# An RWKV-5 attention with a squared-ReLU feed-forward: the bonus term and the state's share of y computed in another way from unit 8, and the order written anew

## The chip, the cores and the metric

One Trainium2 chip, of which the kernel uses one core. The metric is the time of one execution on the device in microseconds (us). The profile is of one execution; its time is given beside its span, which runs from the first to the last instruction.

## The reference

```python
batch, n_heads, seq, head_dim = (4, 8, 768, 48)      # r, k, v; w and u are (heads, head_dim)
...
def _attn_ref(r, k, v, w, u):
    for t in range(S):
        kt, vt, rt = (k[:, :, t].copy(), v[:, :, t].copy(), r[:, :, t].copy())
        cur = np.einsum('bhd,bhe->bhde', u[None] * kt, vt)
        y[:, :, t] = np.einsum('bhd,bhde->bhe', rt, state + cur)
        state = w[None, :, :, None] * state + np.einsum('bhd,bhe->bhde', kt, vt)
...
def _moe_ref(x, w_in, w_out):                        # x is y as (3072, 384)
    h = x @ w_in                                     # w_in is (384, 2048)
    r = np.maximum(h, 0.0)
    g = r * r
    return (g @ w_out).astype(np.float32)            # w_out is (2048, 384)
```

The state of each head is a 48 x 48 matrix that decays by `w` at each step. The bonus term lets a token see itself with the weight `u`: it is the sum over d of r x u x k, one number for each token and head (the "diagonal sum"), times v.

## The kernel before

The sequence is cut into 6 chunks of 128 tokens; a chunk of one batch is a unit, 24 in all, numbered chunk by chunk with the four batches inside (unit 12 is chunk 3 of batch 0). A unit holds 128 tokens on the partitions and 8 heads of 48 numbers, 384 in all.

What is done for a unit i, by the names of the steps:

- `load` brings r, k and v. `scale` (VectorE) multiplies r and k by powers of w into a padded bf16 tile `rkw`, where each head has 64 places, so that a pair of heads fills 128. `cast_v` (ScalarE) makes v bf16.
- `turn` with `evict_rk` (units 0 to 5, on TensorE and ScalarE) or `turn_dma` (a transposing transfer) turns `rkw` to `rkT`, with the two heads of a pair on partitions 0 to 63 and 64 to 127.
- `at` (TensorE) computes the scores: 8 matmuls, each of 64 rows of the array, into two PSUM banks, even heads in one and odd heads in the other. `ats(i)` does that for units i and i + 1. `mask` (VectorE), two for a unit, reads one of these banks and writes the masked scores `am` as bf16.
- The diagonal sums: `rk` (VectorE) multiplies the turned r and k; four small matmuls in `sums` add it up over the partitions with the weights `uwb`. The same `sums` adds k^T v for the state (not for the last four units).
- `diag_v` (VectorE) multiplies v by the diagonal sums. `state_add`, `state_decay` (VectorE) bring the state up to date in `st32`. `state_cast` (ScalarE), two instructions of 64 partitions, copies it as bf16 into `stb`, whose 128 x 96 blocks have zeros off the diagonal.
- `y_mm` (TensorE): 8 matmuls of the masked scores with v, and from chunk 1 on 4 matmuls of the turned r with `stb`, into one bank. `evict_y` (VectorE) adds `diag_v`'s result and writes y as bf16. `x_turn` with `evict_x` (units 0 to 5) or `x_dma` turns y.
- The feed-forward: `mm1(i, m, s)` is TensorE's product with a part of `w_in`, for one unit (m = 1, 4 steps each) or two (m = 2, 8 steps for both); `relu` (ScalarE) reads the bank; `square` runs on VectorE or ScalarE as its last number says; `mm2(i, q)` is a quarter of the second product; `evict_o` (ScalarE) and `store` bring it out. The last unit's product is cut in two (`mm2_half`).

Nothing schedules this at run time. A long string, `SCHEDULE`, lists the steps in one order, and each engine runs its own instructions in that order; a word such as `ats:12@6,2,5,0` also names the PSUM banks (0 to 7) that the step takes. A bank is free again when its reader is done, and semaphores make the later step wait. `fill` steps are matmuls on constants that keep TensorE busy at the start.

Matmuls stand on `L434` (`mm1`), `L460` (`mm2`), `L475` (`mm2_half`), `L327` (`at`), `L347` and `L352` (`sums`), `L390` and `L396` (`y_mm`), `L310` (`turn`), `L420` (`x_turn`), `L232` (`fill`). On VectorE: `L287` (`scale`), `L319` (`rk`), `L339` (`mask`), `L361` (`diag_v`), `L369` and `L371` (`state_add`), `L375` (`state_decay`), `L405` (`evict_y`), `L453` (`square`). On ScalarE: `L442` (`relu`), `L451` (`square`), `L381` (`state_cast`), `L467` (`evict_o`). GpSimd issues some of the loads and nearly all stores, and computes a few small constants (`L259` among them); the other transfers are issued by SyncE (SP).

## Time and profile before

| | us |
|---|---|
| median of 3 runs | 174.15 |
| lowest, highest | 173.06, 174.81 |
| the profiled execution | 172.5 |
| its span | 170.4 |

The granted clock of TensorE is 1.000 of full speed throughout.

In the lines of the profile, `bank<-vb,am` says that an instruction writes a tile `bank` and reads `vb` and `am`; 128*128 is the part of the array that a matmul uses, and 128x96 the size of what it streams. A group's row gives the number of instructions, their busy time in us, the mean duration of one in ns, and behind the second bar the idle time of the engine before them with what ended it. A row of the timeline begins with the start and the length in us of a run of equal instructions. A row of waits gives total us, how often, and the longest. A row of the windows gives the stretch, its length, then the busy time of PE, PEld (the loading of weights), DVE (VectorE), ACT (ScalarE) and POOL (GpSimd), each with its count of instructions, and at last the clock, the share of the transfers and their GB/s.

### The profile page before, as it was taken

The numbers are of one execution on the slowest core, as the hardware profiler recorded it, in microseconds if no ns is written. First come the engines' busy times: TensorE is split into PE (matmuls) and PEld (weight loads), VectorE is DVE, ScalarE is ACT, GpSimd is POOL, SyncE is SP. The second block draws the span as 40 slices with busy tenths as digits, with TensorE's granted clock in tenths as the row PEclk, the third lists the DMA queues.
The fourth block names the chain that finished last, engine by engine and source line by source line (L and its number), as shares of the span: only waits on it lengthen the run. The fifth ranks groups of instructions, "written<-read, shape, count | busy, mean of one in ns | idle before, by whom it ended". The sixth has DMA issues, their size and how long they took to land.

```text
span 170.4 us, 4781 instructions
## 1 busy us (share of the span) xinstructions
PE 163.4 (96%) x1917; PEld 129.9 (76%) x1917; DVE 137.0 (80%) x297; ACT 120.9 (71%) x253; POOL 30.5 (18%) x62
## 2 busy tenths in 40 slices
PE   3899999999999999999999999999999999999993
PEld 2467998778778786795796895896898776999662
DVE  5359969969998999799988979988999898664800
ACT  3355489997685988579499499599359985295830
POOL 7989540000000500001100001203000030030010
PEclk9999999999999999999999999999999999999999
DMA  6999999989999999998999994998989994150014
GB/s 115 188 220 211 221 248 244 227 155 129 187 159 187 209 237 133 192 207 131 250 203 116 200 217 81 251 192 176 252 100 212 197 159 139 27 162 0 4 63 167
DMA packets 94784, 28.83 MB, mean 169 GB/s; under 512 B 90665, under 2 KB 92714, under 8 KB 94762
## 3 DMA queue, kind: packets, MB, share of 16 engines
q1 hardware_dynamic: 90512, 19.08, 73.9%
q0 software_dynamic: 4224, 9.44, 21.4%
q8 instruction: 15, 0.25, 0.6%
q14 instruction: 7, 0.06, 0.2%
q10 hardware_dynamic: 26, 0.00, 0.0%
HBM read 20.45 MB, written 4.72 MB: 148 GB/s over the span
## 4 chain that ended last, share of the span: by engine, by line
PE 84%; DVE 6%; DMA 5%; issue 1%; ACT 1%; ACTq 1%; DVEq 0%
PE bank L434 35%; PE bank L460 31%; PE bank L327 4%; DMA xT<-yb 3%; PE bank L390 3%; DMA rkT<-rkw 2%; PE bank L352 2%; PE bank L232 2%; PE bank L396 2%; PE bank L310 2%; PE bank L475 2%; DVE am L339 1%; DVE rkw L287 1%; PE bank L347 1%; DVE g L453 1%
## 5 line engine op out<-in xcount | busy, mean ns | idle before, releaser
L442 ACT ACTIVATE gr<-bank 128x512 f32<-128x512 f32 x96 | 53.1, 603 | 27.3 <-PE bank L434 25.9
L434 PE MATMUL bank<-xT,w_in_q 128*128 128x128 bf16 (+1 forms) x768 | 70.8, 246 | 0.6 <-DMA xT<-yb 0.4
L460 PE MATMUL bank<-w_out_q,g 128*128 128x384 bf16 x368 | 68.1, 327 | 0.1
L434 PEld LDWEIGHTS <-w_in_q 128*128 128x128 bf16 x768 | 64.2, 113 | 3.4 <-DMA xT<-yb 0.5
L460 PEld LDWEIGHTS <-g 128*128 128x128 bf16 x368 | 33.7, 98 | 19.2 <-DVE g L453 0.6
L453 DVE TENSOR_TENSOR g<-gr 128x512 bf16<-128x512 f32 x49 | 32.4, 686 | 6.9 <-ACT gr L442 6.8
L494 POOL DMA_DIRECT2D out_dram<-osb x21 | 11.3, 543 | 129.4 <-ACT osb L467 118.7
L339 DVE TENSOR_TENSOR am<-bank,smask 128x512 bf16<-128x512 f32 x48 | 31.4, 685 | 2.9 <-PE bank L327 2.8
L451 ACT ACTIVATE g<-gr 128x512 bf16<-128x512 f32 x47 | 29.1, 638 | 0.6
L287 DVE TENSOR_TENSOR rkw<-ldk,wneg 128x384 bf16<-128x384 f32 x24 | 13.2, 553 | 4.8 <-ACT wneg L240 3.6
L381 ACT CAST stb<-st 64x192 bf16<-64x192 f32 x40 | 13.9, 348 | 2.6 <-DVE st L375 2.3
L361 DVE TENSOR_TENSOR dv<-vb,bank 128x384 f32<-128x384 bf16 x24 | 13.0, 550 | 2.4 <-PE bank L352 1.5
L405 DVE TENSOR_TENSOR yb<-bank,dv 128x384 bf16<-128x384 f32 x24 | 13.3, 555 | 1.3 <-PE bank L396 0.3
L287 DVE TENSOR_TENSOR rkw<-ldr,wpos 128x384 bf16<-128x384 f32 x24 | 13.1, 553 | 1.0 <-DMA ldr<-in_r_dram 0.8
L319 DVE TENSOR_TENSOR rk<-rkT 128x512 bf16<-128x512 bf16 x24 | 10.0, 420 | 3.8 <-ACT rkT L314 2.0
L467 ACT COPY osb<-bank 128x384 f32<-128x384 f32 x23 | 10.5, 483 | 2.7 <-PE bank L460 2.7
L291 ACT CAST vb<-ldv 128x384 bf16<-128x384 f32 x24 | 12.1, 512 | 0.4 <-DMA ldv<-in_v_dram 0.3
L371 DVE TENSOR_TENSOR st<-bank,st 64x192 f32<-64x192 f32 x32 | 11.2, 351 | 1.2 <-PE bank L352 0.9
L232 PE MATMUL bank<-warm 128*128 128x256 bf16 x39 | 9.2, 334 | 2.0 <-DVE warm L183 1.5
L314 ACT COPY rkT<-bank 128x512 bf16<-128x512 bf16 x12 | 6.9, 595 | 3.7 <-PE bank L310 3.6
L390 PEld LDWEIGHTS <-am 128*128 128x128 bf16 x192 | 7.9, 96 | 2.0 <-issue 0.7
L327 PEld LDWEIGHTS <-rkT 64*128 64x128 bf16 x192 | 5.5, 96 | 4.2 <-issue 3.9
(58 smaller groups left out, 112.2 us busy)
## 6 DMA issues: line engine op xcount, KB each, us to landing
ldk<-in_k_dram SPq DMA_DIRECT2D x22, 192.0 KB, 4.6
out_dram<-osb POOLq DMA_DIRECT2D x21, 192.0 KB, 3.3
ldr<-in_r_dram SPq DMA_DIRECT2D x20, 192.0 KB, 3.7
ldv<-in_v_dram SPq DMA_DIRECT2D x19, 192.0 KB, 4.3
w_in_q<-in_moe_w_in_dram POOLq DMA_DIRECT2D x4, 384.0 KB, 8.9
w_out_q<-in_moe_w_out_dram POOLq DMA_DIRECT2D x4, 384.0 KB, 10.7
ldv<-in_v_dram POOLq DMA_DIRECT2D x5, 192.0 KB, 9.0
ldr<-in_r_dram POOLq DMA_DIRECT2D x4, 192.0 KB, 8.2
```

The costliest lines, as they stand in the source:

```text
L232: nc.tensor.matmul(out=banks[given.pop(0)][:, :n], lhsT=warm[:, :128], rhs=warm[:, :n], start=True, stop=True)
L287: nc.vector.tensor_tensor(t["rkw"][:, x, :, :, :D], pair(src), pair(wx), ALU.mult)
L339: nc.vector.tensor_tensor(am, t["at"][o], smask.unsqueeze(1).to_broadcast([C, HP, C]), ALU.mult)
L361: nc.vector.tensor_tensor(t["dv"], t["vb"], t["d"].unsqueeze(2).to_broadcast([C, H, D]), ALU.mult)
L381: nc.scalar.copy(stb[b][sl, :, o * D : (o + 1) * D], st32[b][sl])
L390: nc.tensor.matmul(out=y[:, 2 * p + o, :], lhsT=t[f"am{o}"][:, p, :], rhs=t["vb"][:, 2 * p + o, :], start=(o == 0 and p == 0), stop=c == 0 ...
L405: nc.vector.tensor_tensor(t["yb"], t["y"], t["dv"].rearrange("p h d -> p (h d)"), ALU.add)
L434: nc.tensor.matmul(out=t["h", s][:, a], lhsT=turned, rhs=chunks[c]["xT"][:, n, b : b + m, :], start=(n == 0), stop=(n == NK - 1),)
L442: nc.scalar.activation(t["gr", s], t["h", s], AF.Relu)
L451: nc.scalar.activation(g, x, AF.Square)
L453: nc.vector.tensor_tensor(g, x, x, ALU.mult)
L460: nc.tensor.matmul(out=t["o"], lhsT=chunks[units[i][0]]["g"][:, f, units[i][1], :], rhs=w_out_q[f // 4][:, f % 4, :], start=(f == 0), stop ...
```

## The change

From unit 8 on three things are computed in another way.

- The diagonal sums leave TensorE. `product` (VectorE) multiplies the scaled r and k in bf16 as they stand before the turn; `weigh` (GpSimd) multiplies that by u x w, spread over all partitions by two new loads (`wide_load`) and one product (`wide_product`); `fold` (GpSimd), twice, adds halves, 48 to 24 to 12 numbers a head; `head_sums` (VectorE) adds up the 12. `rk` and the four small matmuls of `sums` go.
- The state's share of y is computed inside `ats`, straight behind the scores: 16 matmuls for the two units, each of 64 rows and 48 columns, in place of 4 for a unit of 128 rows and 96 columns. Even and odd heads go to two banks, which the two units share, so `ats` takes six banks rather than four. `ys` later adds the masked scores' share for both units, and `evict_y` reads the two banks with two instructions. `state_cast` becomes one instruction of 128 partitions, into `stc`.
- The order is a new one for the whole kernel, from the start. By its words 65 squares run on ScalarE and 31 on VectorE (47 and 49 before), and there are 34 fills (39 before).

Of the string one line before and after, then the code:

```diff
-square:8:2:7:0 ats:12@6,2,5,0 store:5:POOL scale:14:0 mm2:9:2 mask:13:1 turn_dma:14 sums:13@7 mm1:10:2:0@1
...
+weigh:13 evict_o:7 load:17:rt:SP square:8:2:6:1 ats:12@5,7,0,4,3,6 turn_dma:15 square:8:2:7:1 state_decay:11 fold:13:0
...
+    WIDE_FROM = 8
     IN_PIECES, OUT_PIECES = (1, 1)
 
     const = ctx.enter_context(tc.tile_pool(name="const", bufs=1))
-    room = {"g": 2, "rkT": 5, "vb": 8, "rk": 3, "dv": 5, "yb": 4, "xT": 3, "gr": 6, "osb": 4, "am": 4}
+    room = {"pr": 4, "pw": 2, "ds": 4, "g": 2, "rkT": 5, "vb": 8, "rk": 3, "dv": 5, "yb": 4, "xT": 3, "gr": 6, "osb": 4, "am": 4}
     held = {"ldr": 6, "ldk": 8, "ldv": 6}
     pools = {}
 
@@ -218,6 +224,9 @@
     wend_c = const.tile([128, HP], F32)
     wend = wend_c.unsqueeze(2).to_broadcast([128, HP, D])
 
+    stc = [const.tile([128, HP, D], BF16, name=f"stc_{b}") for b in range(B)]
+    wide = [const.tile([128, H, D], F32, name=f"wide{x}") for x in range(2)]
+
     w_in_q = [const.tile([128, NK, dff // NQ], BF16, name=f"w_in_q{q}") for q in range(NQ)]
     w_out_q = [const.tile([128, NF // NQ, dm], BF16, name=f"w_out_q{q}") for q in range(NQ)]
 
@@ -312,6 +321,33 @@
     def evict_rk(i, x):
         t = tiles[i]
         nc.scalar.copy(turned(i)[:, x], t["tp", x])
+
+    def wide_load(x):
+        src = (w, u)[x].rearrange("h d -> (h d)").unsqueeze(0).to_broadcast([128, dm])
+        nc.sync.dma_start(out=wide[x].rearrange("p h d -> p (h d)"), in_=src)
+
+    def wide_product():
+        nc.gpsimd.tensor_tensor(wide[1], wide[1], wide[0], ALU.mult)
+
+    def product(i):
+        t = tiles[i]
+        t["pr"] = buffer("pr", [C, H, D], BF16)
+        nc.vector.tensor_tensor(pair(t["pr"]), t["rkw"][:, 0, :, :, :D], t["rkw"][:, 1, :, :, :D], ALU.mult)
+
+    def weigh(i):
+        t = tiles[i]
+        t["pw"] = buffer("pw", [C, H, D], F32)
+        nc.gpsimd.tensor_tensor(t["pw"], t["pr"], wide[1], ALU.mult)
+
+    def fold(i, n):
+        x = tiles[i]["pw"]
+        m = D >> (n + 1)
+        nc.gpsimd.tensor_tensor(x[:, :, :m], x[:, :, :m], x[:, :, m : 2 * m], ALU.add)
+
+    def head_sums(i):
+        t = tiles[i]
+        t["d"] = buffer("ds", [C, H], F32)
+        nc.vector.tensor_reduce(out=t["d"], in_=t["pw"][:, :, : D // 4], axis=mybir.AxisListType.X, op=ALU.add)
 
     def rk(i):
         t = tiles[i]
@@ -329,9 +365,21 @@
                     start=True, stop=True,
                 )
 
+    def halves(i):
+        return [bank("y", i - i % 2, o).rearrange("p (u x) -> p u x", u=2)[:, i % 2, : dm // 2].rearrange("p (a d) -> p a d", a=HP) for o in range(2)]
+
     def ats(i):
         at(i)
         at(i + 1)
+        for j in (i, i + 1):
+            y = halves(j)
+            for p in range(HP):
+                for o in range(2):
+                    sl = slice(o * 64, o * 64 + 64)
+                    nc.tensor.matmul(
+                        out=y[o][:, p, :], lhsT=tiles[j]["rkT"][sl, 0, p, :], rhs=stc[units[j][1]][sl, p, :],
+                        start=(j == i and p == 0), stop=False, skip_group_check=True,
+                    )
 
     def mask(i, o):
         t = tiles[i]
@@ -342,8 +390,9 @@
         c, b = units[i]
         t = tiles[i]
         t["s"] = bank("s", i)[:, :dm].rearrange("p (a d) -> p a d", a=HP)
-        t["d"] = bank("s", i)[:, dm : dm + H]
-        for p in range(HP):
+        if i < WIDE_FROM:
+            t["d"] = bank("s", i)[:, dm : dm + H]
+        for p in range(HP if i < WIDE_FROM else 0):
             nc.tensor.matmul(
                 out=t["d"], lhsT=t["rk"][:, p, :], rhs=uwb[:, p, :],
                 start=(p == 0), stop=(p == HP - 1 and c == NCH - 1), skip_group_check=True,
@@ -352,7 +401,7 @@
             nc.tensor.matmul(
                 out=t["s"][:, p, :], lhsT=t["rkw"][:, 1, p].rearrange("p o e -> p (o e)"),
                 rhs=t["vb"][:, 2 * p : 2 * p + 2, :].rearrange("p h d -> p (h d)"),
-                start=False, stop=(p == HP - 1), skip_group_check=True,
+                start=(i >= WIDE_FROM and p == 0), stop=(p == HP - 1), skip_group_check=True,
             )
 
     def diag_v(i):
@@ -376,9 +425,22 @@
 
     def state_cast(i):
         b = units[i][1]
-        for o in range(2):
+        if i >= WIDE_FROM - B:
+            nc.scalar.copy(stc[b], st32[b])
+        for o in range(2 if i < WIDE_FROM - B else 0):
             sl = slice(o * 64, o * 64 + 64)
             nc.scalar.copy(stb[b][sl, :, o * D : (o + 1) * D], st32[b][sl])
+
+    def ys(i):
+        for j in (i, i + 1):
+            t = tiles[j]
+            y = halves(j)
+            for p in range(HP):
+                for o in range(2):
+                    nc.tensor.matmul(
+                        out=y[o][:, p, :], lhsT=t[f"am{o}"][:, p, :], rhs=t["vb"][:, 2 * p + o, :],
+                        start=False, stop=j > i and p == HP - 1, skip_group_check=True,
+                    )
 
     def y_mm(i):
         c, b = units[i]
@@ -402,6 +464,12 @@
     def evict_y(i):
         t = tiles[i]
         t["yb"] = buffer("yb", [C, dm], BF16)
+        if i >= WIDE_FROM:
+            out_y = t["yb"].rearrange("c (a o d) -> c o a d", o=2, d=D)
+            dv = t["dv"].rearrange("c (a o) d -> c o a d", o=2)
+            for o, y in enumerate(halves(i)):
+                nc.vector.tensor_tensor(out_y[:, o], y, dv[:, o], ALU.add)
+            return
         nc.vector.tensor_tensor(t["yb"], t["y"], t["dv"].rearrange("p h d -> p (h d)"), ALU.add)
 
     def x_tile(i):
@@ -499,7 +567,8 @@
         evict_rk, evict_x, evict_y, fill, load, mask, mm1, mm2,
         mm2_half, power, relu, rk, scale, spread_columns, spread_log, square,
         state_add, state_cast, state_decay, store, store_half, sums, turn, turn_dma,
-        u_columns, win, wout, x_dma, x_turn, y_mm
+        u_columns, win, wout, x_dma, x_turn, y_mm, ys,
+        product, weigh, fold, head_sums, wide_load, wide_product
     )}
 
     def value(x):
```

More of the change, by code (lines that the diff above doesn't have):

```diff
@@ L108 @@
[L108 to L112 removed]
+load:1:kt:SP load:1:rt:POOL fill@7 load:0:rt:SP 2*fill@7 load:1:vt:POOL fill@7 load:0:kt:SP fill@7 load:2:kt:SP
@@ new lines @@
+relu:10:2:1 mm1:10:2:6@7 evict_y:13 state_cast:11 load:16:rt:SP square:10:2:2:1 mm2:8:1 product:15 x_dma:13
+relu:10:2:0 diag_v:12 mm2:8:2 weigh:15 square:10:2:1:1 evict_y:12 mm1:10:2:4@0 square:10:2:0:1 x_dma:12
+square:10:2:5:0 relu:10:2:6 sums:12@4 mm2:11:0@3 evict_o:9 state_add:12 fold:15:0 sums:13@6 relu:10:2:4 load:17:kt:SP
+mm2:11:1 weigh:14 state_add:13 state_cast:10 load:14:vt:SP relu:10:2:7 mm2:8:3 square:10:2:4:0 square:10:2:6:1
+load:18:kt:SP ats:14@7,1,4,0,6,5 evict_o:8 fold:14:0 load:18:rt:SP cast_v:15 store:6:POOL mm2:10:0@2 mask:15:0
```

187 lines of the change are left out of this document (93 added, 94 removed).

## The prediction

> **What bounds the kernel now.** I read the page first: busy times, then the chain of waits.
>
> ```profile
> span 170.4 us, 4781 instructions
> ...
> PE 163.4 (96%) x1917; PEld 129.9 (76%) x1917; DVE 137.0 (80%) x297; ACT 120.9 (71%) x253; POOL 30.5 (18%) x62
> ...
> PE 84%; DVE 6%; DMA 5%; issue 1%; ACT 1%; ACTq 1%; DVEq 0%
> ```
>
> The kernel is bound by TensorE. A busy PE says little, since a matmul's row covers its latency; what a step costs is the distance to the next step's start. The timeline of PE gives these prices:
>
> ```profile
> 86.86 0.36 PE L390 MATMUL bank<-vb,am 128*128 128x48 bf16 x8
> 87.06 0.33 PE L396 MATMUL bank<-stb,rkT 128*128 128x96 bf16 x4
> 87.23 0.25 PE L347 MATMUL bank<-uwb,rk 128*128 128x8 bf16 x4
> 87.33 0.33 PE L352 MATMUL bank<-vb,rkw 128*128 128x96 bf16 x4
> 87.50 0.81 PE L460 MATMUL bank<-w_out_q,g 128*128 128x384 bf16 x4
> 88.15 0.36 PE L390 MATMUL bank<-vb,am 128*128 128x48 bf16 x8
> ...
> 88.52 0.82 PE L434 MATMUL bank<-xT,w_in_q 128*128 128x256 bf16 x6
> 89.17 1.50 PE L460 MATMUL bank<-w_out_q,g 128*128 128x384 bf16 x8
> ...
> 93.21 0.62 PE L327 MATMUL bank<-rkT 64*128 64x128 bf16 x16
> 93.76 1.47 PE L460 MATMUL bank<-w_out_q,g 128*128 128x384 bf16 x8
> ```
>
> So y from the masked scores costs 0.20 us (86.86 to 87.06), y from the state 0.17, the four small diagonal matmuls 0.10, the state sums 0.17, an `mm2` quarter 0.65, an `mm1` step of two units 0.65, an `ats` 0.55. The start gives the rest, and the last row where PE ends:
>
> ```profile
> 19.45 0.83 PE L434 MATMUL bank<-xT,w_in_q 128*128 128x128 bf16 x12
> 20.12 0.33 PE L420 MATMUL bank<-identb,yb 128*128 128x128 bf16 x3
> 20.29 0.39 PE L310 MATMUL bank<-identb,rkw 128*128 128x128 bf16 x4
> 20.51 2.17 PE L434 MATMUL bank<-xT,w_in_q 128*128 128x128 bf16 x36
> ...
> 24.18 0.40 PE L327 MATMUL bank<-rkT 64*128 64x128 bf16 x8
> 24.51 0.30 PE L434 MATMUL bank<-xT,w_in_q 128*128 128x128 bf16 x2
> ...
> 164.79 2.80 PE L475 MATMUL bank<-w_out_q,g 128*128 128x256 bf16 x32
> ```
>
> An `mm1` step of one unit is 0.67 us, an `x_turn` 0.17, a `turn` 0.22, a single `at` 0.33. Useful work by counts of the steps: `mm1` 32 x 0.67 + 64 x 0.65 = 63.0; `mm2` 92 x 0.65 + 2.8 for the two halves = 62.6; `at` 8 x 0.33 + 8 x 0.55 = 7.0; diagonal and sums 24 x 0.10 + 20 x 0.17 = 5.8; y 24 x 0.20 + 20 x 0.17 = 8.2; turns 12 x 0.22 + 6 x 0.17 = 3.7. Together 150.3 of 170.4. PE ends at 167.6, so 2.8 is the tail. By 20.12 only 6 us of useful work is done (three units' turns, scores, sums and y, three `mm1` steps), so 14 is the start. That leaves about 3 us lost in the 147 us between: a new order can win hardly more than that there. Who is next in line is told by one long window:
>
> ```profile
> 60.00:140.00 80.00, 79.38 (x885) 63.63 (x883) 72.58 (x152) 62.46 (x133) 6.25 (x12) 1.00 1.11 184
> ```
>
> The columns after the length are PE, PEld, DVE, ACT and POOL busy. VectorE has 7.4 us free in these 80; it feeds PE through the masks.
>
> **The change part by part.** *PE.* Per pair from unit 8, two times 0.10 (diagonal) and two times 0.17 (state y) go: 0.54 us. In come 16 matmuls of 64 rows and 48 columns. The nearest row is `at`, also 64-row tiles: the second eight of an `ats` add 0.55 - 0.33 = 0.22, 27.5 ns each, so 16 x 27.5 = 0.44 us. The bounds are half of that, 0.22, if two row tiles of 48 columns share a slot, and a whole `ats`, 0.55. Saving per pair 0.10 (from -0.01 to 0.32), times 8: **-0.8 us** (+0.1 to -2.6). I keep 0.44, since `L390` with the same 48 columns also starts every 25 ns. The Trainium skill, "TensorE: Matmul & The Clock Gate", Part 3, says that matmuls in different row groups run together, starting about 4 ns apart; by that rule the 16 would be eight slots and the saving the upper one. The trace agrees in so far as the 128-column tiles of `at` come every 27.5 ns, and shows no 48-column row tile.
>
> *VectorE and ScalarE.* The groups:
>
> ```profile
> L453 DVE TENSOR_TENSOR g<-gr 128x512 bf16<-128x512 f32 x49 | 32.4, 686 | 6.9 <-ACT gr L442 6.8
> ...
> L451 ACT ACTIVATE g<-gr 128x512 bf16<-128x512 f32 x47 | 29.1, 638 | 0.6
> ...
> L381 ACT CAST stb<-st 64x192 bf16<-64x192 f32 x40 | 13.9, 348 | 2.6 <-DVE st L375 2.3
> ...
> L405 DVE TENSOR_TENSOR yb<-bank,dv 128x384 bf16<-128x384 f32 x24 | 13.3, 555 | 1.3 <-PE bank L396 0.3
> ...
> L319 DVE TENSOR_TENSOR rk<-rkT 128x512 bf16<-128x512 bf16 x24 | 10.0, 420 | 3.8 <-ACT rkT L314 2.0
> ...
> L371 DVE TENSOR_TENSOR st<-bank,st 64x192 f32<-64x192 f32 x32 | 11.2, 351 | 1.2 <-PE bank L352 0.9
> ...
> L375 DVE TENSOR_TENSOR st<-st,wend_c 128x192 f32<-128x192 f32 x16 | 5.6, 352 | 0.1
> ```
>
> Per unit from 8: `rk` goes (0.42). `product` comes, 384 bf16 elements: 0.36, between three quarters of `rk` (0.31) and `L405`'s 0.55 for 384 elements at full width. `head_sums` reads 96 elements: 0.25, at most `L375`'s 0.35. `evict_y` becomes two instructions of 192 elements: 2 x 0.351 against 0.555, +0.15. Net +0.34 x 16 = +5.4. `diag_v` stays at 384 elements. By the counts 18 squares leave VectorE (49 to 31): -18 x 0.66 = -11.9. So VectorE loses 6.5 (137.0 to about 130.5). ScalarE gets the 18 at 0.62 (29.1 / 47), +11.1, and casts 16 states in one instruction instead of two; `L375` against `L371` shows that 64 and 128 partitions cost the same, so -16 x 0.348 = -5.6: 126.4. Neither reaches PE; both are covered by PE's work as a sum. In units 8 to 21 VectorE has 10 squares less and 14 x 0.34 more: its 7.4 us of room become about 9.
>
> *GpSimd.* Per unit one product of 384 elements and two adds of 192 and 96. The trace has no such row; the nearest, by groups and by line (least, median and longest duration):
>
> ```profile
> masks.py:199 POOL TENSOR_SCALAR_AFFINE_SELECT identb<-identb 128x128 bf16<-128x128 bf16 x1 | 0.3, 292 | 0.1
> ```
> ```profile
> L259 POOL TENSOR_TENSOR wend_c<-wend_c x6: 192/198/470, 11.9 to 13.5; 128x4 f32<-128x4 f32 x6
> ```
>
> A product of four elements takes 198 ns (the median), a one-input operation on 128 takes 292: (292 - 198) / 124 = 0.76 ns an element. An estimate of twice that for two inputs, on 0.2 fixed, gives 0.78, 0.49 and 0.35: 1.6 us a unit, 26 in all (17 by the one-input rate, 35 by three times it). GpSimd goes from 30 to about 57 of 170, and it also issues the stores, so a store waiting for its `evict_o` holds up the weighting behind it. `head_sums` stands in VectorE's queue and waits for GpSimd; behind it stand squares, `scale`, `product` and `evict_y`. This is the place, pair 12 and 13 on VectorE, before:
>
> ```order
> L339 TENSOR_TENSOR am1_1722<-bank0_61,smask_134 128x512
> L375 TENSOR_TENSOR st32_3_139<-st32_3_139,wend_c_148 128x192
> L339 TENSOR_TENSOR am1_1741<-bank2_63,smask_134 128x512
> L339 TENSOR_TENSOR am0_1752<-bank5_66,smask_134 128x512
> L319 TENSOR_TENSOR rk_1762<-rkT_1519 128x512
> L361 TENSOR_TENSOR dv_1767<-vb_1671,bank7_68 128x384
> ```
>
> and now, `ds` being the head sums and `pw` what GpSimd wrote:
>
> ```order
> L424 TENSOR_TENSOR st32_3_139<-st32_3_139,wend_c_148 128x192
> L387 TENSOR_TENSOR am0_1772<-bank0_61,smask_134 128x512
> L387 TENSOR_TENSOR am1_1781<-bank7_68,smask_134 128x512
> L387 TENSOR_TENSOR am0_1789<-bank5_66,smask_134 128x512
> L387 TENSOR_TENSOR am1_1800<-bank4_65,smask_134 128x512
> L350 TENSOR_REDUCE ds_1811<-pw_1729 128x8
> L521 TENSOR_TENSOR g_1584<-gr_1809 128x2x256
> ```
>
> The four masks moved together, straight behind `ats`, and the wait on GpSimd stands behind them. That order is needed: `ats:12` takes six banks (5, 7, 0, 4 and 3, 6 for y), while 1 and 2 hold `mm2` results, so the next `mm1` has no bank until a mask has read one. PE's cover is one `mm2` quarter, 0.65.
>
> *An added wait.* The state y now stands in `ats`, so the cast of the state must be done before the masks rather than after. ScalarE before, with the cast of batch 0 for unit 12:
>
> ```order
> L451 ACTIVATE g_973<-gr_1305 128x4x128
> L381 CAST stb_0_140<-st32_0_136 64x4x48 x2
> L442 ACTIVATE gr_1379<-bank3_64 128x512
> L442 ACTIVATE gr_1424<-bank5_66 128x512
> L442 ACTIVATE gr_1439<-bank3_64 128x512
> ```
>
> and now:
>
> ```order
> L510 ACTIVATE gr_1709<-bank0_61 128x512
> L535 COPY osb_1719<-bank4_65 128x384
> L429 CAST stc_0_149<-st32_0_136 128x192
> L535 COPY osb_1731<-bank6_67 128x384
> L519 ACTIVATE g_1584<-gr_1709 128x2x256
> ```
>
> The cast moved behind an output's copy, and only one `mm2` quarter and the 0.55 of the scores lie between it and its reader. Everything on PE is queued behind that reader. I cost it at nothing while ScalarE keeps up, and at what it is late otherwise.
>
> *The start.* The third unit's `x_turn` stands behind two `mm1` steps, before behind three (0.67 less done). VectorE's early work hangs on the same transfer as before:
>
> ```profile
> 11.16 0.56 DVE L287 TENSOR_TENSOR rkw<-ldr,wpos 128x384 bf16<-128x384 f32 x1 [0.83 <-DMA ldr<-in_r_dram]
> ```
>
> and now has `scale:1:0`, `scale:0:1` and `scale:2:1` behind it by then, so less is left: I take half back. **+0.3 us** (-0.4 to +0.7). The two broadcast loads are of 192 KB each, beside 72 loads of that size: nothing, unless a transpose behind them is waited for.
>
> **Sum.** -0.8 + 0.3, and the 3 us lost in the middle stay: span 169.9, the profiled execution's 172.5 us become 172.0. The median of the runs, 174.15, lies 1.65 above that execution, so I forecast **173.7 us**, no change. One per cent, 1.74 us, is about what a measurement of this kernel can tell from none. Chance 0.37.
>
> **The rivals.** *Slower: GpSimd and VectorE keep each other out.*
>
> ```profile
> 12.84 0.55 DVE L287 TENSOR_TENSOR rkw<-ldk,wneg 128x384 bf16<-128x384 f32 x1
> 12.97 0.47 POOL L259 TENSOR_TENSOR wend_c<-wend_c 128x4 f32<-128x4 f32 x1
> ```
>
> This GpSimd operation took 0.47 us, the median of its six equals 198 ns: it began inside a VectorE operation with two SBUF inputs and ended at 13.44, 0.05 after that one (13.39). Now 48 GpSimd operations of 0.35 to 0.78 us run there, mean 0.54. If a little over half of one is waited each time, 48 x 0.3 = 14 us fall on VectorE, against 9 of room: 5 us of late masks, 178.7. It decides from 9 / 48 = 0.19 us a time. Against it: in the order the instruction behind most of them on VectorE is a mask, `state_add` or `evict_y`, which read PSUM. Chance 0.25. The Trainium skill, "SBUF — State Buffer", section "Who interferes with whom", has the rule: a VectorE instruction with two SBUF inputs and a GpSimd one that reads SBUF exclude each other for the whole instruction. By that rule the row above is no accident; the trace agrees with GpSimd as the loser and does not show VectorE as one.
>
> *Slower: late casts.* If ScalarE, 5.5 us busier, is late by 0.4 at each of 8 pairs, PE loses 3.2: 176.9. ScalarE had 17 us free in the window above, so 0.10.
>
> *Faster: fewer waits in the middle.* These transfers were waited for:
>
> ```profile
> DVE rk L319 <- DMA rkT<-rkw: 1.6, 2, 1.1
> PEld L434 <- DMA xT<-yb: 0.5, 1, 0.5
> ```
>
> If an order with longer transfers assumed takes 1.5 of the 3 us lost, and the row tiles cost the lower bound (-2.6), with +0.3: -3.8 at most, likely -2.5: 171.6. Chance 0.28; for it speaks VectorE's load, 6.5 us lower, against it that only some 2 us of waits on transfers can be seen.
>
> **The numbers.** Faster 0.28, within 1% 0.37, slower 0.25 + 0.10 = 0.35. The range runs from 170.5 (3.8 off) to 178.7 (the first rival): one in ten is left out on each side.
>
> **What would show it.** PE: 16 row tiles behind the scores in 0.44 us. VectorE about 130, ScalarE about 126, GpSimd near 57. Right if PE's idle time between 20 us and its end stays near 1 us; the first rival shows as GpSimd or VectorE operations stretched by each other and PE `L502` waiting for `am`; the second as PE `L379` waiting for `stc`. Wrong if the lost time comes from neither, for instance from transposes waited for.

## The result, and the profile after

| | before | after |
|---|---|---|
| median, us | 174.03 (4 runs) | 176.81 (4 runs) |
| lowest, highest | 173.06, 174.81 | 176.28, 177.62 |
| the profiled execution | 172.5 | 176.28 |
| its span | 170.4 | 174.5 |

The change made the kernel slower: the ratio of the times, after to before, is 1.025, 95% interval 1.020 to 1.030. The forecast was 173.7 us, no change.

The page of the kernel after, with the span, the busy times and the shares of the chain of waits:

```profile
span 174.5 us, 4859 instructions
...
PE 162.2 (93%) x1912; PEld 126.9 (73%) x1912; DVE 134.6 (77%) x311; ACT 123.2 (71%) x255; POOL 64.8 (37%) x111
...
PE 70%; DVE 17%; DMA 5%; issue 3%; ACT 2%; ACTq 1%; SPq 0%; DVEq 0%
```

TensorE has less to do and is less often what the end waits for (70% of the chain, 84% before); VectorE's share went from 6% to 17%. The saving on TensorE is there, and larger than forecast. The timeline of PE after, at the scores of units 12 and 13:

```profile
85.19 0.62 PE L363 MATMUL bank<-rkT 64*128 64x128 bf16 x16
85.64 0.36 PE L379 MATMUL bank<-stc,rkT 64*128 64x48 bf16 x16
85.94 0.82 PE L528 MATMUL bank<-w_out_q,g 128*128 128x384 bf16 x4
```

From the scores to the next step it is 0.75 us, 0.20 more than before, for work that cost 0.54 in its old form: 0.34 saved for a pair, 2.7 us for eight. So the span, 4.1 us longer, hides 6.8 us lost. Where they are lost shows when the useful work that stands ahead of each `at` or `ats` in the order (the prediction's prices, 0.75 for the new `ats`) is taken from the time at which it starts. The table is worked out from the starts in the timelines; "halves" is the first matmul of `mm2_half`. The last four columns are experiments told below.

```
lost us at    before  after | x2     x15    x18    x9
at:3           14.1   16.1  | 16.1   14.7   15.3   16.6
at:4           14.3   17.4  | 16.6   16.6   17.1   17.9
at:7           14.6   18.1  | 17.4   17.7   18.0   18.6
ats:8          14.7   18.8  | 17.5   18.3   19.4   19.7
ats:12         15.8   21.4  | 18.9   22.0   20.5   21.4
ats:16         16.7   21.8  | 19.5   22.4   20.9   23.3
ats:22         17.1   23.1  | 19.9   23.4   21.9   25.2
halves         17.2   23.3  | 20.7   23.7   22.1   25.5
```

Read downwards, a column that stays level loses nothing there. After loses 3.1 us more than before up to the scores of unit 4 (36 us), 2.5 more from there to those of unit 12 (85 us), 0.5 in the 83 us that follow, and 0.8 behind `halves` (6.4 to the end, 5.6 before). That makes 6.9, the same as the 6.8 but for rounding. Other executions with this order start up to 0.9 us worse (the repeat, x10: 18.3 at `at:4`), so the split is good to about that.

The new way of computing begins with unit 8. Nearly all of the loss lies ahead of it or at its first four units, and from `ats:12` on, where all of the new way runs, next to nothing is lost. The first loss is seen by the first scores. The timelines of PE, before:

```profile
7.54 0.61 PE L310 MATMUL bank<-identb,rkw 128*128 128x128 bf16 x4
...
8.15 1.06 PE L310 MATMUL bank<-identb,rkw 128*128 128x128 bf16 x8
...
9.79 0.61 PE L327 MATMUL bank<-rkT 64*128 64x128 bf16 x8
```

and after:

```profile
7.52 0.61 PE L319 MATMUL bank<-identb,rkw 128*128 128x128 bf16 x4 [0.72 <-DVE rkw L296]
...
8.46 0.61 PE L319 MATMUL bank<-identb,rkw 128*128 128x128 bf16 x4
...
9.73 0.61 PE L319 MATMUL bank<-identb,rkw 128*128 128x128 bf16 x4
...
10.34 0.64 PE L319 MATMUL bank<-identb,rkw 128*128 128x128 bf16 x4
...
10.98 0.63 PE L319 MATMUL bank<-identb,rkw 128*128 128x128 bf16 x4
...
11.97 0.61 PE L363 MATMUL bank<-rkT 64*128 64x128 bf16 x8
```

Before, three turns stand ahead of the scores of unit 1; after, five, unit 0's two first. VectorE likewise scales r of unit 0 first. Everything of unit 1 is 2.2 us late.

For the second stretch the waits of PE between 20 and 90 us after name a transfer:

```profile
PE bank L502 <- DMA xT<-yb: 1.6, 2, 1.1
PE bank L396 <- DVE rk L355: 0.4, 1, 0.4
```

And GpSimd and VectorE do stretch each other. The groups after:

```profile
L521 DVE TENSOR_TENSOR g<-gr 128x512 bf16<-128x512 f32 x31 | 22.7, 747 | 11.9 <-ACT gr L510 11.8
...
L471 DVE TENSOR_TENSOR yb<-bank,dv 128x192 bf16<-128x192 f32 x32 | 9.7, 351 | 4.2 <-PE bank L440 4.1
...
L335 DVE TENSOR_TENSOR pr<-rkw 128x384 bf16<-128x384 bf16 x16 | 6.6, 420 | 0.1
L424 DVE TENSOR_TENSOR st<-st,wend_c 128x192 f32<-128x192 f32 x16 | 6.5, 408 | 0.1
```
```profile
L340 POOL TENSOR_TENSOR pw<-pr,wide 128x384 f32<-128x384 bf16 x16 | 16.2, 1014 | 49.4 <-DVE pr L335 48.5 <-DVE ds L350 0.9
...
L345 POOL TENSOR_TENSOR pw<-pw 128x192 f32<-128x192 f32 x16 | 10.7, 672 | 0.7
L345 POOL TENSOR_TENSOR pw<-pw 128x96 f32<-128x96 f32 x16 | 7.2, 460 | 0.4
```

A square takes 747 ns (686 before), a `state_decay` 408 (352).

So there were two theories to begin with: the order of the first units is at fault (A), or GpSimd's hold on VectorE (B). The letters that follow in the expectations are theories named there, each with the time that it gives.

### The profile page after: what moved, and what is told of

The parts are those of the page before. It is cut to its first block, busy times and chain, and to the rows that moved or that the text cites. A ratio compares the mean times of both kernels' runs of the same rounds, so it can differ in the third digit from the quotient of the medians.

```text
span 174.5 us, 4859 instructions
## 1 busy us (share of the span) xinstructions
PE 162.2 (93%) x1912; PEld 126.9 (73%) x1912; DVE 134.6 (77%) x311; ACT 123.2 (71%) x255; POOL 64.8 (37%) x111
## 4 chain that ended last, share of the span: by engine, by line
PE 70%; DVE 17%; DMA 5%; issue 3%; ACT 2%; ACTq 1%; SPq 0%; DVEq 0%
PE bank L502 30%; PE bank L528 26%; DMA xT<-yb 5%; DVE rkw L296 4%; PE bank L363 3%; DVE am L387 3%; DVE dv L410 2%; PE bank L319 2%; PE bank L440 2%; PE bank L543 2%; DVE yb L473 1%; DVE st L420 1%; DVE g L521 1%; DVE yb L471 1%; PE bank L401 1%
## 5 line engine op out<-in xcount | busy, mean ns | idle before, releaser
L510 ACT ACTIVATE gr<-bank 128x512 f32<-128x512 f32 x96 | 54.5, 602 | 25.5 <-PE bank L502 21.2
L519 ACT ACTIVATE g<-gr 128x512 bf16<-128x512 f32 x65 | 39.7, 638 | 0.4
L340 POOL TENSOR_TENSOR pw<-pr,wide 128x384 f32<-128x384 bf16 x16 | 16.2, 1014 | 49.4 <-DVE pr L335 48.5
L521 DVE TENSOR_TENSOR g<-gr 128x512 bf16<-128x512 f32 x31 | 22.7, 747 | 11.9 <-ACT gr L510 11.8
L296 DVE TENSOR_TENSOR rkw<-ldr,wpos 128x384 bf16<-128x384 f32 x24 | 14.1, 592 | 5.4 <-ACT wpos L249 3.6
L345 POOL TENSOR_TENSOR pw<-pw 128x192 f32<-128x192 f32 (+1 forms) x32 | 17.8, 566 | 1.1
L296 DVE TENSOR_TENSOR rkw<-ldk,wneg 128x384 bf16<-128x384 f32 x24 | 13.9, 590 | 0.5 <-DMA ldk<-in_k_dram 0.4
L471 DVE TENSOR_TENSOR yb<-bank,dv 128x192 bf16<-128x192 f32 x32 | 9.7, 351 | 4.2 <-PE bank L440 4.1
L363 PE MATMUL bank<-rkT 64*128 64x128 bf16 x192 | 8.5, 222 | 0.2 <-DMA rkT<-rkw 0.2
L410 DVE TENSOR_TENSOR dv<-vb,ds 128x384 f32<-128x384 bf16 x16 | 8.5, 553 | 0.1
```

The source lines that it names most:

```text
L296: nc.vector.tensor_tensor(t["rkw"][:, x, :, :, :D], pair(src), pair(wx), ALU.mult)
L340: nc.gpsimd.tensor_tensor(t["pw"], t["pr"], wide[1], ALU.mult)
L345: nc.gpsimd.tensor_tensor(x[:, :, :m], x[:, :, :m], x[:, :, m : 2 * m], ALU.add)
L363: nc.tensor.matmul(out=t["at"][o][:, p, :], lhsT=t["rkT"][sl, 1, p, :], rhs=t["rkT"][sl, 0, p, :], start=True, stop=True,)
L410: nc.vector.tensor_tensor(t["dv"], t["vb"], t["d"].unsqueeze(2).to_broadcast([C, H, D]), ALU.mult)
L510: nc.scalar.activation(t["gr", s], t["h", s], AF.Relu)
```

## The experiments

Ratios are to the kernel before, timed beside it on the same chip, with 95% intervals. In the edits a line of the order is cut to what moves; the PSUM banks were dealt out anew where a join needed it.

**The kernel after, again (x10).** No edit.

> The kernel after, unchanged, on the same chip as the three runs beside it, as the measure for them: both theories 1.025, within 0.5%.

1.025 (1.020 to 1.030). This is the measure for the rest.

### GpSimd and VectorE

**Without GpSimd's work (x4).**

```diff
-        t["pw"] = buffer("pw", [C, H, D], F32)
-        nc.gpsimd.tensor_tensor(t["pw"], t["pr"], wide[1], ALU.mult)
+        t["pw"] = t["pr"]
...
-        nc.gpsimd.tensor_tensor(x[:, :, :m], x[:, :, :m], x[:, :, m : 2 * m], ALU.add)
```

> The changed kernel without the products and the folds on GpSimd: the head sums read 12 of the 48 unweighted numbers, so the bonus term is not the reference's. VectorE then waits for no GpSimd operation and shares nothing with it. Theory A: 176.3 us (0 to 1 below the changed kernel). Theory B: 174 us or less, and VectorE's squares back from 747 to 686 ns.

1.021 (1.017 to 1.026). Its page, and the same groups:

```profile
span 174.5 us, 4804 instructions
...
PE 162.1 (93%) x1912; PEld 127.3 (73%) x1912; DVE 129.3 (74%) x311; ACT 123.3 (71%) x255; POOL 31.4 (18%) x63
```
```profile
L521 DVE TENSOR_TENSOR g<-gr 128x512 bf16<-128x512 f32 x31 | 20.9, 687 | 12.5 <-ACT gr L510 12.3
...
L424 DVE TENSOR_TENSOR st<-st,wend_c 128x192 f32<-128x192 f32 x16 | 5.6, 351 | 0.1
L335 DVE TENSOR_TENSOR pr<-rkw 128x384 bf16<-128x384 bf16 x16 | 5.5, 351 | 0.1
```

The squares are back at 687 ns, so the stretching is GpSimd's doing: 5.3 us of VectorE (134.6 to 129.3). But the span is the same 174.5. The hold is real and costs next to nothing here; B falls as the cause.

**Weighing twice (x5).**

```diff
         nc.gpsimd.tensor_tensor(t["pw"], t["pr"], wide[1], ALU.mult)
+        spare = buffer("px", [C, H, D], F32)
+        nc.gpsimd.tensor_tensor(spare, t["pr"], wide[1], ALU.mult)
```

> The kernel after with the weighing done twice, the second time into a tile that nobody reads: 16 more GpSimd instructions of 1.0 us. Theory B (GpSimd's hold on VectorE costs time as such; after's GpSimd work of 34 us cost 0.7 us by x4): another 16 us cost another 0.3 to 0.7 us, 1.027 to 1.03. Its rival (the hold is hidden until VectorE is full; in after VectorE is idle 20 us of 174): 1.025 and no more, with squares on VectorE longer than 747 ns. If the chain product, weigh, folds and head sums becomes late, 1.04 or more, with waits of VectorE for GpSimd in the trace.

1.036 (1.029 to 1.043), 1% above after. Of its waits:

```profile
DVE ds L352 <- POOL pw L347: 5.2, 6, 1.3
```

VectorE now waits for GpSimd in its queue, six times; in after there was no such wait of note. GpSimd is busy 17.5 us longer than in after, and that costs 1.8 us, where the first 33 us (64.8 less the 31.4 of x4) cost at most 0.7. The waits point at the chain through GpSimd as what is close to its limit. The run doesn't separate that from VectorE's instructions, which got longer too (busy 138.2 us, a square 768 ns).

### The start

**The new start under the old kernel (x2), and only its part up to the first `mm1` (x16).** x2 has the order of after up to `at:3`, x16 up to the first `mm1`, and the kernel before behind it, with the old way throughout. Up to the first `mm1` the two orders differ in the order of the turns, and in that of scalings, powers of w, fills and loads.

```diff
-power:1 spread_columns@1 power:0 scale:1:1 win:1:0 fill@7 scale:1:0 fill@7 turn:1:1@2
-scale:0:0 fill@0 load:5:kt:SP evict_rk:1:1 turn:1:0@3 u_columns turn:0:0@4
+power:0 fill@7 power:1 scale:0:0 win:1:0 scale:1:1 turn:0:0@1
+load:3:kt:POOL scale:0:1 fill@0 load:5:kt:SP scale:1:0 turn:0:1@2
```

> The kernel before, with the order of the changed one up to and with the scores of unit 3, then the order of before; no step of the change itself. Theory A: 174.0 + 3.1 = 177.1 us. Theory B: 174.0 us, since GpSimd computes nothing new.

> The reverse: the order of after up to the first big product, and then the order of before with the old way throughout. Theory G: 1.4 us slower than before, 1.008. Theory H (the loss comes after the first big product): 1.0 to 1.003. All of the 3.5 us of x2 (1.02): then the turns alone set the start.

x2: 1.020 (1.017 to 1.024), 3.5 us. x16: 1.024 (1.017 to 1.031). The timeline of PE in x16, its first two scores, and its first `mm1` with what stands just ahead of it:

```profile
11.99 0.61 PE L327 MATMUL bank<-rkT 64*128 64x128 bf16 x8
14.37 0.40 PE L327 MATMUL bank<-rkT 64*128 64x128 bf16 x8
...
18.74 0.37 PE L390 MATMUL bank<-vb,am 128*128 128x48 bf16 x8 [0.65 <-DVE am L339]
18.95 0.84 PE L434 MATMUL bank<-xT,w_in_q 128*128 128x128 bf16 x12
```

`at:1` is 2.2 us late and the first `mm1` 2.5 (16.48 before). By the time, 1.024, G (1.008) and H (1.0 to 1.003) both miss, and the third case of the expectation is met: the order ahead of the first `mm1` is enough for all that x2 costs. Neither kernel holds an instruction of the new way. Two limits go with that. The edit moves the whole of this stretch, so the turns are the likeliest part of it, as `at:1` stands behind five of them instead of three, but not the only one. And x16's first `mm1` is 1.05 us later than in after (17.90): at the join a `y_mm` stands ahead of it and waits 0.65 us for a mask (the row at 18.74), so about 1 us of the 2.5 belongs to the join. In after the first `mm1` is 1.4 late, as G reckoned.

**The old start under the new kernel: up to `at:3` (x1), or up to the first `mm1` (x15).** The edit is the reverse of the one above.

> The changed kernel with the order of before up to and with the scores of unit 3 (some 25 us), then its own order; nothing else differs. Theory A, the new order of the first units is late: by 25 us the changed kernel had lost 3.1 us more of TensorE's time than before, so this gives 176.8 - 3.1 = 173.7 us. Theory B, GpSimd and VectorE keep each other out from unit 8: nothing of that changes, 176.8 us.

> The order of before up to the first big product (16.5 us), and from there the order of after with the new way from unit 8. Theory G (the turns of unit 0 ahead of those of unit 1 cost the start: 1.4 us of the 3.1 are there when the first big product runs): 1.025 less 1.4 us, so 1.017. Theory H (the rest of the start, or what follows it, takes that back): 1.022 to 1.03.

x1: 1.029 (1.021 to 1.036); x15: 1.021 (1.016 to 1.027). x1 misses A. Its table shows that it loses the 2 us won just behind the join (14.1 at `at:3`, 17.3 at `at:4`) and 3.7 more between `ats:8` and `ats:10`, where after loses 1.2 (the granted clock of this execution was 0.66 there, from 65 to 70 us). x15 lies between G and H by its time; its trace shows the start won and then lost again. The timeline of PE in x15, its first scores, first `mm1` and the `mm1` steps that follow `at:3`:

```profile
9.77 0.58 PE L364 MATMUL bank<-rkT 64*128 64x128 bf16 x8
...
16.22 0.86 PE L503 MATMUL bank<-xT,w_in_q 128*128 128x128 bf16 x12
...
27.89 0.83 PE L503 MATMUL bank<-xT,w_in_q 128*128 128x128 bf16 x12
...
33.64 1.50 PE L503 MATMUL bank<-xT,w_in_q 128*128 128x128 bf16 x24
```

The same steps in after begin at 11.97, 17.90, 28.96 and 34.51. The 2.2 us won are 1.7 at the first `mm1`, 1.1 at 28 us and 0.9 at 34: most of the head start goes little by little, ahead of 28 us. Against before, x15 is only 0.6 worse at `at:3` and 2.3 at `at:4`; on that stretch the new order has five fills and four turns on TensorE, where before has products of the feed-forward.

What is left of the head start goes at one place, the first `mm1` of unit 8. The timelines of PE there, first in after, then in x15, then in x18 (below), which has the start of x15 and two loads moved besides:

```profile
75.35 3.46 PE L502 MATMUL bank<-xT,w_in_q 128*128 128x256 bf16 x36 [1.06 <-DMA xT<-yb]
```
```profile
75.91 3.45 PE L503 MATMUL bank<-xT,w_in_q 128*128 128x256 bf16 x36 [2.30 <-DVE ds L351]
```
```profile
73.81 3.45 PE L503 MATMUL bank<-xT,w_in_q 128*128 128x256 bf16 x36
```

In x15 TensorE stands 2.3 us ahead of this step, in after 1.06, in x18 not at all. So x15 starts earlier than after and is 0.6 us later here. The row of x15 names VectorE's head sums, which this step doesn't read, and the masks that freed its bank had ended by 74.77. Likelier it is again the transposes of y, for the two of them come late in x15 as SP shows (x15, then after):

```profile
69.27 4.14 SPq L483 DMA_TRANSPOSE xT<-yb  x2
```
```profile
69.39 2.53 SPq L482 DMA_TRANSPOSE xT<-yb  x2
```

The later one lands at 75.78 in x15 and at 75.21 in after, and the `mm1` starts 0.13 and 0.14 us behind it. By this reading two losses cover each other: whoever takes away only the late start waits longer for the transposes.

### The new way in the old order, and the old way in the new

**The order of after with the old way in it (x9).** `rk` and the diagonal's matmuls come back behind `ats`, `y_mm` and the half casts at their places; GpSimd only stores.

```diff
-state_decay:11 fold:13:0 mask:13:0 mm2:9:3 weigh:12 load:15:vt:SP mask:12:1
+state_decay:11 rk:12 rk:13 dsum:12 dsum:13 mask:13:0 mm2:9:3 load:15:vt:SP mask:12:1
```

> The other corner: the order of after, word for word, with the old way of computing in it: sums of the diagonal on TensorE behind the attention matmuls, y in one bank a unit by the old matmuls, nothing on GpSimd but stores. Theory A: the order's loss stays and the saving goes, so 1.025 + 2.4/174 = 1.035 to 1.04. Theory C: without the new operations nothing is late, so 1.00 to 1.01.

1.048 (1.044 to 1.052). A was right in sign and C wrong, and it is worse than the saving explains. Up to `ats:12` it loses as much as after (21.4 both), so a loss of this size comes with the order, whichever way is computed. But it is made of other waits: x9 never waits for a transpose of y there, and waits for squares instead (0.6 and 0.3 us). Its queue on SP lacks the two broadcast loads of the new way, and two transposes of y are issued at 53.89 and 59.09 in it, at 56.00 and 60.70 in after; so the waits of after for transposes can't be put down to the order alone. Behind `ats:12`, where after stays nearly level, x9 loses 4.1 us more (after 1.9): the order of after is fitted to the new way and slow with the old.

**The diagonal alone (x6) and both parts (x8) in the order of before.** `weigh`'s tile has four buffers here instead of two.

```diff
-mask:10:1 turn_dma:12 mm1:8:2:4@7 mask:11:1
+mask:10:1 turn_dma:12 product:12 weigh:12 fold:12:0 fold:12:1 mm1:8:2:4@7 mask:11:1
```

> The kernel before, its order kept word for word, with only the diagonal sums taken to VectorE and GpSimd from unit 8: product, weighing and folds stand behind the transpose of their unit, head_sums ahead of diag_v, rk and the four TensorE sums go, y stays as it was. Theory A (the order of the first 64 us is at fault, and the new operations are worth what TensorE no longer does): TensorE's work falls by 16 x 4 x 0.026 = 1.7 us, so 0.99 of the time before. Theory C (the new operations cost time wherever they stand, since the diagonal now passes over three engines and makes VectorE late): 1.005 or more.

> As the run before it, and y from row tiles as well, with the state part and the masked part of one unit issued together where the kernel before issued y; still the order of before, except that three instructions wait for a bank. Theory A: TensorE's work falls by about 2.4 us, so 0.985 of the time before. Theory C: 1.01 or more, as slow as the order of after.

x6: 1.065 (1.060 to 1.071); x8: 1.085 (1.079 to 1.092). Here C is right: the new way without its order is far worse than with it. The 100 us from 60 on, in x6 and in after:

```profile
60.00:160.00 100.00, 92.37 (x987) 71.84 (x985) 92.23 (x184) 69.66 (x148) 40.79 (x58) 1.00 0.84 161
```
```profile
60.00:160.00 100.00, 97.90 (x1115) 77.71 (x1113) 84.51 (x192) 73.03 (x154) 41.77 (x65) 1.00 0.91 168
```

VectorE, the third figure, is busy 92 us of 100 in x6 and 85 in after. The new order gives ScalarE 18 squares; without that, VectorE is as busy as TensorE (92.23 and 92.37 us). Whether that is what costs the time, the next run asks.

**x8 with 18 squares given to ScalarE (x11).**

```diff
-square:8:2:2:0 mm2:9:0@7 x_dma:10 relu:8:2:5
+square:8:2:2:1 mm2:9:0@7 x_dma:10 relu:8:2:5
```

> The kernel x8 (both parts of the new way in the order of before, 1.085) with 18 of the squares of units 8 to 23 moved from VectorE to ScalarE at their places, so that VectorE has 31 squares as in the kernel after. Theory D (the new way costs VectorE time and what made x6 and x8 slow is VectorE, busy 92 of the 100 us from 60 to 160; the order of after hides that by giving 18 squares to ScalarE): the time falls from 1.085 by at least 0.05, to 1.03 or less, and if the new way's 2.4 us of TensorE come out, to 0.99. Theory E (it is the chain over three engines that is late, whatever VectorE's load): 1.07 or more.

1.067 (1.063 to 1.072). VectorE's load explains a fifth of x8's loss; D's numbers are missed, E's 1.07 is nearer. That the chain over three engines is late would fit, but no run shows it by itself; about 2 us are likely the broadcast loads (x13, below), and the rest stays open.

### Joins in the middle

**The order of before, and the new way in its own order from unit 8 (x3, x12), 12 (x13) or 16 (x14).** x3 and x12 differ in one place:

```diff
-relu:5:1:2 wide_product store:2:POOL scale:10:0 scale:10:1 load:11:kt:SP
+relu:5:1:2 wide_product store:2:POOL load:11:kt:SP
...
+scale:10:0 scale:10:1 sums:8@1 weigh:9 evict_o:4 turn_dma:10 product:10
```

> The changed kernel with the order of before up to the scores of units 8 and 9 (some 55 us), with the two new loads put among the loads there, then its own order. Theory A, both orders losing what was read from the traces: the difference in lost time at that point is 4.7 us, so 176.8 - 4.7 = 172.1 us, below both kernels, with the joint costing up to 1 us. Theory B: 176.8 us.

> The kernel x3 with the scaling of unit 10 put behind the sums of unit 8, so that VectorE no longer stands 5 us for a load at the join of the two orders: the order of before through unit 7, that of after from unit 8 with all of the new way. Theory A (what the order of the first 64 us loses is the whole loss): 172, ratio 0.99 to 1.0. Rival F (the new way needs the head start that the order of after gives its first units, and pays later): 1.02 or more.

> The order and the way of before through unit 11, to the decay of unit 10's state (about 85 us), and from there the order of after with the whole of the new way for units 12 to 23; at this place the two orders have done nearly the same, and three scalings and loads at the join are sorted by hand. Theory A (from 80 us on the new way in its own order loses no more than the kernel before, and all of the loss lies in the order of the first 80 us): TensorE's work falls by 12/16 of 2.4 = 1.8 us, the tail costs 0.75, so about 1 us less than before, 0.994, and up to 1.003 if the join costs 1.5 us. Rival F (the new way pays in the second half too, but the order of after has stored up a head start for it in the first): 1.015 or more.

> The same with the join four units later, at the second product of unit 13 (about 108 us), and the new way for units 16 to 23: theory A: work less by 8/16 of 2.4 = 1.2 us, tail 0.75, so 0.997, and up to 1.006 with a join that costs 1.5 us. Rival F: 1.01 or more.

1.046 (1.042 to 1.049), 1.042 (1.038 to 1.047), 1.055 (1.051 to 1.059) and 1.031 (1.026 to 1.036): all miss A, and the tables of x3, x12 and x13 put the loss at the join. In x3 the lost time goes from 14.6 at `at:7` to 25.2 at `ats:8` and then to 27.4 at `halves`: 10.6 us at the join, and 2.2 in the 104 us behind it. In x12 the join costs 9.7. Two orders that agree on which steps are done still disagree on which are under way: in x3 VectorE stands 5.1 us for r of unit 10, and in x12, with that mended, still 3.8 us for a load. A part of both is no matter of the join: each also waits some 2.2 us for a transpose of y behind the broadcast loads, which x13 shows by itself. The windows of x12 there (PE first, the granted clock before the last two figures):

```profile
55.00:60.00 5.00, 2.28 (x16) 1.40 (x17) 1.20 (x4) 1.34 (x4) 3.23 (x5) 0.60 1.04 186
60.00:65.00 5.00, 3.00 (x31) 3.00 (x31) 3.30 (x9) 3.56 (x8) 0.00 (x0) 0.50 1.25 210
```

x13 shows something else before its join: 4.5 us are lost by `ats:10`, where it still runs the old way in the old order, with one thing added, the two broadcast loads. (Its order leaves out `wide_product`, so behind the join it weighs by u alone and GpSimd has one product less; that bears on nothing ahead of the join.) SP's timeline in x13:

```profile
51.82 0.57 SPq L326 DMA_DIRECT2D wide<-in_u_dram  x1
52.43 0.45 SPq L326 DMA_DIRECT2D wide<-in_w_dram  x1
52.92 1.06 SPq L274 DMA_DIRECT2D ldr<-in_r_dram  x2
54.03 3.07 SPq L274 DMA_DIRECT2D ldv<-in_v_dram  x1
57.20 1.37 SPq L481 DMA_TRANSPOSE xT<-yb  x1
```

and PE's:

```profile
63.27 0.93 PE L501 MATMUL bank<-xT,w_in_q 128*128 128x128 bf16 x12 [2.30 <-DMA xT<-yb]
```

The transpose of y is issued at 57.20, where before issues it at 54.78, and TensorE waits 2.3 us for it. Behind this hole the granted clock is halved for 3.4 us:

```profile
63.90:67.30 3.40, 3.40 (x39) 2.72 (x37) 2.10 (x5) 0.60 (x1) 0.00 (x0) 0.50 1.29 205
```

As an estimate from the clock, 1.7 of these 3.4 us are lost, so the hole and the clock make about 4 of the 4.5 us. So these loads are not free when a transpose stands behind them; x6 has 2.0 us of the same wait between 45 and 60 us, which is part of its loss at `ats:8`. The join proper costs x13 another 8.4.

So these runs don't give the kernel that A promised. But x3, x12 and x13 repeat the table's other finding: behind the join, with all of the new way, the columns are nearly level (2.2, 2.3 and 1.5 us until `halves`).

### The transfers, and several losses at once

**Two loads behind the transposes of y (x17); the same with the old turns of x15 (x18); and without GpSimd's work besides (x19).**

```diff
-load:13:rt:SP x_dma:7
+x_dma:7 load:13:rt:SP
...
-load:13:kt:SP ... x_dma:9 ... x_dma:8
+x_dma:9 ... x_dma:8 load:13:kt:SP
```

> The kernel after, with the loads of r and k of unit 13 moved on SP from ahead of the transposes of y of units 7 and 9 to behind those of 7 and 8. If the two waits of TensorE for those transposes (0.52 us at 64.8 us and 1.06 us at 75.4 us) come from the queue, each falls by about 0.6 us, the length of a load's issue, and the ratio falls from 1.025 to about 1.019. If the transposes are late for another reason (their y is late, or they take 4 us by themselves), 1.025.

> The kernel x15 (old order up to the first big product, then the new one) with the two loads of x17 moved as well. Theory P (the losses of the new order stand side by side and hide each other): the two together give more than their sum alone, 1.012 to 1.016. Theory Q (something that none of the runs has touched holds the new order until 90 us): 1.02 to 1.025, and the lost time at 95 us is 20.8 as in every other run with this order.

> x18 with the weighing and the folds left out besides, so that the bonus term is not the reference's (the head sums add 12 of 48 unweighted products): Theory P: 1.005 to 1.01. Theory Q: 1.018 or more.

x17: 1.023 (1.018 to 1.028). Its waits of PE between 20 and 90 us:

```profile
PE bank L396 <- DVE rk L355: 0.9, 1, 0.9
...
PE bank L502 <- DMA xT<-yb: 0.2, 1, 0.2
```

The waits for the transposes went from 1.6 to 0.2 us, as its expectation said, and the span is 174.6 (174.5 in after), which it didn't. x17 is 0.8 better than after at `ats:12`, but from there to `ats:16` it loses 1.8 (22.4), after 0.4. One wait that is new there:

```profile
106.95 2.38 PE L528 MATMUL bank<-w_out_q,g 128*128 128x384 bf16 x12 [0.58 <-DVE yb L471]
```

Another, of 0.26 us for a mask, stands at 86.19; together they are 0.8. x15's span is 174.5 too. With both changes, x18:

```profile
span 172.8 us, 4872 instructions
```

The span is 1.7 us less where each alone gave none; by times x18 is at 1.017 (1.011 to 1.022), after at 1.025, 1.4 us. The times don't decide between P and Q: 1.017 lies between P's 1.012 to 1.016 and Q's 1.02 to 1.025, the intervals of x15, x17 and x18 overlap, and x19 at 1.021 (1.016 to 1.026) is what Q said. The traces speak for P (losses that hide each other): x15's head start goes at the wait near 75 us, shown above, and x17's gain at the waits just named, while x18 has neither and is still at 20.9 at `ats:16` (22.4 in both x15 and x17). x18 is the best kernel found with the new way; it doesn't reach the kernel before.

## Why the prediction was wrong

- **TensorE's work, -0.8.** Right in kind, off in size: -2.7, at the bound of -2.6. "I keep 0.44" failed; the 16 row tiles lengthen `ats` by 0.20 us. The lower bound of 0.22, two row tiles of 48 columns in one slot, was the better choice. The Trainium skill's "TensorE: Matmul & The Clock Gate", Part 3, says that tiles in different row groups run together. The trace agrees with that as far as the net cost goes (0.20); from their own start to the next step the 16 tiles take 0.30 us, 85.64 to 85.94.
- **The start, +0.3 (at most +0.7).** This is the first step that failed. The prediction compared only the `mm1` steps ahead of the third `x_turn`, and held that VectorE "hangs on the same transfer as before". It did not look at what now stands ahead of the first scores: the scaling of r and two turns of unit 0 were put ahead of unit 1's, and `at:1` starts at 11.97 instead of 9.79. By its own prices after has lost 1.1 us more than before at the third `x_turn`, 1.9 at `at:3` and 3.1 at `at:4`, and this start alone makes the old kernel 3.5 us slower (x2; x16 reaches as much with the part ahead of the first `mm1`, about 1 us of it from the join).
- **"The 3 us lost in the middle stay."** Before loses 2.9 from `at:4` to `halves`, as reckoned; after loses 5.9 there. This step failed too, in the new order's stretch from 36 to 85 us, where after loses 4.0. What makes these is only partly found. TensorE's waits there that a trace shows come to 2.2 us: 1.6 for transposes of y, which the prediction named as what would make it wrong, 0.4 for `rk` and 0.2 for a turned `rkT`. Its idle time between 20 us and its end, which was to stay near 1 us, is 3.3 (0.6 before). x17 takes most of the 1.6 away and the time hardly moves. x9, without any of the new way, loses 3.5 on the same stretch, but at other waits.
- **VectorE 130.5, ScalarE 126.4, GpSimd 57.** Measured 134.6, 123.2 and 64.8. Without the stretching VectorE has 129.3 (x4), so the counts were right; GpSimd's prices were too low (0.78, 0.49 and 0.35 against 1.01, 0.67 and 0.46).
- **First rival, GpSimd and VectorE, 0.25.** The mechanism is real and did not decide. The prediction set the point at 0.19 us for each of 48 GpSimd instructions; x4 shows 5.3 / 48 = 0.11. The Trainium skill, "SBUF — State Buffer", section "Who interferes with whom", says that a VectorE instruction with two SBUF inputs and a reading GpSimd one keep each other out, and that one with at most one SBUF input, outside the two-port modes, does not contend. The trace agrees, now with VectorE as the loser as well: squares and decays, with two SBUF inputs, are stretched from 687 to 747 and from 351 to 408 ns (x4 and after); `evict_y`, which reads PSUM and one SBUF tile, stays at 351 ns. x5 shows what comes next: VectorE waits for the sums.
- **The two broadcast loads, "nothing, unless a transpose behind them is waited for".** The condition was the right one: in x13 one is, for 2.3 us. In after their share isn't separated: the transposes of y are 2.1 and 1.6 us later in its queue than in x9, which has no such loads, and yet x9 loses the same up to `ats:12`.
- **Second rival, late casts.** PE waited 0.2 us at `L379` in all; it did not happen.
- **Third rival, faster.** From `ats:12` on the new kernel does keep the gain in work. The losses ahead of it ate that and 4 us more.
- **Small sums.** GpSimd's bounds come out as 17.8 and 34.1 us rather than 17 and 35, and the low end of the range as 170.4 rather than 170.5. Nothing hangs on them.

The forecast failed on the order, which the prediction read at the places of the new way and took as unchanged elsewhere. That 176.8 lies inside the stated range is luck: its upper end, 178.7, was made from the first rival, which did not decide.

What stays open: what makes the rest of the 4.0 us from 36 to 85 us, which part of the order ahead of the first `mm1` costs how much, the tail's 0.8 us, which no run touched, and whether an order exists that has the old start and the new way at no cost. x18 suggests that part of the loss can be undone by hand.

## What to carry to other kernels

When a change brings a new order for the whole program, price the order as a change of its own: compare the first scores, the first big product and a few marks along the way on each engine, from the first instruction on, and ask at each what now stands ahead of it. Transplant in both directions (new order with old work, old order with new work): here the one costs 4.8%, the other 8.5% and both together 2.5%, so neither work nor order can be judged apart from the other. A loss that a profile shows is not yet a price: three suspects were taken away singly, and none gave more than 0.4%. Two of them covered each other at one later wait, so take suspects away in pairs too, and look where an earlier start is lost again.

## What the runs showed of the hardware

- 16 matmuls of 64 rows and 48 columns take 0.30 us of TensorE's time, 19 ns each, where matmuls of 64 rows and 128 columns came every 27.5 ns and full-height ones of 48 columns every 25.
- GpSimd's two-input operations took 1.01 us for 384 elements a partition, 0.67 for 192 and 0.46 for 96, while sharing with VectorE: by estimate from these three, about 2 ns an element on a fixed 0.25 us.
- After holes of 2.2 us (x12) and 2.3 us (x13) in TensorE's work its granted clock was 0.50 for the next 3.4 us and more (rows above); after holes of 2.3 us in x15 and 2.4 us in x11 it stayed at 1.00. While it was 0.50, four matmuls of `mm2` in x12 took 1.30 us instead of 0.65. The Trainium skill's "TensorE: Matmul & The Clock Gate", Part 1, gives half rate after at least one idle window of about 3.4 us. The half rate agrees; the holes here were shorter than that window.
